# The first four heads of an attention and mixer kernel loaded in pairs, k and q side by side in the partitions; last output chunk in columns of 384 and 128

## The chip, the cores and the metric

The kernel runs on one core of one Trainium2 chip. The metric is device time in microseconds (us). Some kernels here also show a slower state, with a lower granted TensorE clock, and fast runs are compared only with fast runs. In the profile the engines are PE (TensorE matmul), PEld (its weight load), ACT (ScalarE), DVE (VectorE), POOL (GpSimd) and SP (SyncE); "SPq" and "ACTq" are their sequencers, which issue transfers.

## The reference

Block-causal attention (8 batches, 8 heads, 576 positions, 64 columns per head, blocks of 64), then a mixer layer over tokens and one over channels:

```python
scores = 1 / sqrt(64) * q @ k.T          # masked where the query's block is before the key's
x = softmax(scores) @ v                  # heads put side by side: 8 x 576 x 512
h = relu(x.transpose(0, 2, 1) @ w_tok1) @ w_tok2
u = x + h.transpose(0, 2, 1)
out = u + relu(u @ w_ch1) @ w_ch2        # w_ch1 512 x 1536
```

## The kernel before

The program is a list of operations with dependencies and estimated costs. A search with a seeded random generator picks an order, which is then emitted; each engine works through its own list. Only what the change touches is shown.

The first four heads of k and q are loaded as float32 by the two hardware queues (SP and ACT), cast to bf16, and transposed in 32x32 blocks by VectorE. All later ones come through POOL's software queue, which casts on the way.

```python
def load_qk(b, hg, after=[]):
    first = b == 0 and hg == 0
    parts = ((0, NB // 2), (NB // 2, NB))          # two halves of the columns
    for n, (src, raw, dst) in enumerate(((k, kraw[i], kT[i]), (q, qraw[i], qT[i]))):
        hbm = src[b, 4 * hg : 4 * hg + 4].rearrange("h (p k) d -> (h p) (k d)", p=32)   # 4 heads = 128 partitions
        st = stage[0][:, 1152 * n : 1152 * (n + 1)]
        ...
        for f, (k0, k1) in enumerate(parts):
            if first:                              # 128 x 576 floats: 288 KB
                queue.dma_start(out=st[:, D * k0 : D * k1], in_=hbm[:, D * k0 : D * k1])   # SP or ACT
                cast(o, raw2[:, D * k0 : D * k1], st[:, D * k0 : D * k1])                  # ACT or DVE
            nc.vector.transpose(dst..[:, k0:k1], raw2..[:, k0:k1])                         # 128 x 288 int32
```

(The emit functions are shown inlined.) The first score group covers all four heads at once; heads 2 and 3 use two spare PSUM banks and are read by two exps of 512 columns. While TensorE waits in the head of the kernel, small matmuls on zeros ("fillers") keep it busy:

```python
P.add("PE", WARM * 0.36, emit, ...)               # 16 matmuls of 512 columns on zeros
for n in range(KEEP):                             # fillers of 256 columns, used if a gap allows
    P.add("PE", 0.11, emit, ..., at=5.0 + 0.12 * n, until=20.0, quick=True)
```

The last output chunk is computed, added and stored in two parts:

```python
for cols in (slice(0, 256), slice(256, 512)) if last else (slice(0, 512),):
    ...  # 12 matmuls into a bank, add of u by DVE, store by SP
```

The softmax here doesn't subtract the row's maximum and nothing guards it: scores larger than these inputs give would overflow.

## Time and profile before

| | before |
|---|---|
| time, three runs | 307.05 us median (306.29 to 307.42) |
| span of the profiled run | 304.3 us |
| PE busy, share of the chain of waits | 98%, 95% |
| first score, first exp, first channel matmul | 8.24, 8.92, 26.82 |
| PE end, end of the span | 300.96, 304.26 |

The timeline of the queue of ACT shows the cost of issuing; the columns are start, length, engine, line, operation, destination <- source, count, and in brackets the idle time before it and what ended it:

```profile
0.74 0.41 ACTq L380 DMA_DIRECT2D gT<-in_k_dram  x1
1.18 0.46 ACTq L380 DMA_DIRECT2D gT<-in_q_dram  x1
1.67 1.28 ACT L344 ACT_TABLE_LOAD   x1 [1.67 <-PEq L1139]
```

ACT issues two loads at about 0.44 each, then loads its table. The staging buffer bears the name gT, whose memory it borrows. The view by stretches of time has, for each stretch, the busy time of five engines with their instructions, the granted clock, the busy share of the DMA engines (packet times added up, so it can exceed 1), and GB/s:

```profile
2.00:3.50 1.50, 1.50 (x5) 0.61 (x4) 1.16 (x6) 1.15 (x2) 1.50 (x3) 1.00 0.92 313
3.50:5.00 1.50, 1.50 (x7) 0.59 (x5) 0.43 (x3) 0.20 (x1) 1.50 (x4) 1.00 1.00 383
5.00:7.00 2.00, 2.00 (x15) 1.21 (x14) 1.39 (x3) 1.85 (x4) 2.00 (x4) 1.00 1.29 175
```

The four loads move at 383 GB/s between 3.5 and 5. After that the rate is 175 GB/s.

### The profile page before, as it was taken

The numbers are of one execution on the slowest core, as the hardware profiler recorded it, in microseconds if no ns is written. First come the engines' busy times: TensorE is split into PE (matmuls) and PEld (weight loads), VectorE is DVE, ScalarE is ACT, GpSimd is POOL, SyncE is SP. The second block draws the span as 40 slices with busy tenths as digits, with TensorE's granted clock in tenths as the row PEclk, the third lists the DMA queues.
The fourth block names the chain that finished last, engine by engine and source line by source line (L and its number), as shares of the span: only waits on it lengthen the run. The fifth ranks groups of instructions, "written<-read, shape, count | busy, mean of one in ns | idle before, by whom it ended". The sixth has DMA issues, their size and how long they took to land.

```text
span 304.3 us, 7056 instructions
## 1 busy us (share of the span) xinstructions
PE 296.9 (98%) x2999; PEld 160.7 (53%) x3034; DVE 155.5 (51%) x380; ACT 164.6 (54%) x233; POOL 62.1 (20%) x96
## 2 busy tenths in 40 slices
PE   8999999999999999999999999999999999999995
PEld 4575456465454564555554564645446545555443
DVE  5566539989595599584987253615023021010112
ACT  5887855677855756875557856324413503615300
POOL 9766454702610602600140000000000000000000
PEclk9999999999999999999999999999999999999999
DMA  8999999995982998975193002033113222100133
GB/s 202 179 196 209 200 191 187 220 216 91 142 121 44 161 119 139 189 46 60 54 107 88 2 2 53 18 95 97 36 32 140 46 80 49 43 26 2 69 138 106
DMA packets 64383, 31.94 MB, mean 105 GB/s; under 512 B 53088, under 2 KB 55008, under 8 KB 64352
## 3 DMA queue, kind: packets, MB, share of 16 engines
q0 software_dynamic: 44320, 17.34, 48.9%
q1 hardware_dynamic: 19744, 13.57, 17.1%
q10 hardware_dynamic: 288, 0.59, 0.5%
q8 instruction: 23, 0.38, 0.5%
q14 instruction: 8, 0.07, 0.1%
HBM read 35.85 MB, written 9.44 MB: 149 GB/s over the span
## 4 chain that ended last, share of the span: by engine, by line
PE 95%; DMA 2%; issue 1%; DVE 1%; ACT 0%; ACTq 0%
PE mm L1031 31%; PE mm L947 28%; PE mm L555 10%; PE sc L508 10%; PE mm L736 6%; PE mm L829 4%; PE mm L974 4%; DMA gT<-in_q_dram 2%; PE mm L860 1%; PE mm L332 1%; PE mm L780 0%; PE mm L910 0%; DVE qT L393 0%; PE mm L1023 0%; PE mm L765 0%
## 5 line engine op out<-in xcount | busy, mean ns | idle before, releaser
L527 ACT ACTIVATE e_sb<-sc 128x1024 bf16<-128x1024 f32 x95 | 92.5, 1028 | 26.3 <-PE sc L508 24.5
L947 PE MATMUL mm<-uT,wc_sb 128*128 128x512 bf16 x384 | 91.2, 380 | 0.1
L1031 PE MATMUL mm<-wc_sb,gT 128*128 128x512 bf16 (+1 forms) x372 | 89.4, 372 | 1.5 <-issue 0.5
L722 ACT ACTIVATE gT<-mm 128x512 bf16<-128x512 f32 x74 | 44.2, 597 | 63.1 <-PE mm L947 62.8
L947 PEld LDWEIGHTS <-wc_sb 128*128 128x128 bf16 x384 | 41.9, 114 | 39.3 <-issue 3.9
L1031 PEld LDWEIGHTS <-gT 128*128 128x128 bf16 x396 | 36.9, 98 | 40.8 <-issue 3.3
L1056 DVE TENSOR_TENSOR o_sb<-mm,u_sb 128x512 f32<-128x512 f32 (+1 forms) x29 | 19.5, 672 | 74.5 <-PE mm L1031 74.3
L422 POOL DMA_DIRECT2D v<-in_v_dram x45 | 37.2, 839 | 35.3 <-PE sc L508 23.6
L508 PE MATMUL sc<-qT,kT 32*128 32x64 bf16 (+4 forms) x744 | 35.4, 281 | 0.5 <-DVE qT L393 0.5
L555 PEld LDWEIGHTS <-e_sb 128*128 128x128 bf16 x896 | 31.1, 97 | 8.0 <-issue 3.6
L555 PE MATMUL mm<-v,e_sb 128*128 128x65 bf16 x896 | 33.9, 193 | 0.1
L583 DVE TENSOR_TENSOR x_sb<-mm,rinv 128x320 bf16<-128x320 f32 x64 | 31.0, 491 | 2.0
L724 DVE TENSOR_SCALAR gT<-mm 128x512 bf16<-128x512 f32 x22 | 15.2, 689 | 15.9 <-PE mm L947 15.7
L844 DVE TENSOR_TENSOR u_sb<-mm,x_sb 128x512 bf16<-128x512 f32 x28 | 18.0, 686 | 10.2 <-PE mm L829 9.0
L393 DVE STREAM_TRANSPOSE qT<-qraw 128x288 int32<-128x288 int32 x32 | 21.6, 706 | 3.0 <-PE sc L508 2.1
L393 DVE STREAM_TRANSPOSE kT<-kraw 128x288 int32<-128x288 int32 x32 | 20.9, 703 | 4.3 <-DMA kraw<-in_k_dram 1.7
L508 PEld LDWEIGHTS <-kT 32*128 32x128 bf16 x752 | 12.3, 93 | 19.8 <-issue 16.7
L736 PE MATMUL mm<-x_sb,w_sb 128*128 128x512 bf16 (+1 forms) x98 | 18.0, 314 | 0.3
L533 DVE MEMSET e_sb<- 64x128 uint32 (+1 forms) x72 | 10.5, 153 | 14.7 <-ACT e_sb L527 11.4
L373 POOL DMA_DIRECT2D qraw<-in_q_dram x15 | 8.3, 552 | 42.2 <-DVE qT L393 28.5
L577 DVE RECIPROCAL rinv<-mm 128x5 f32<-128x5 f32 x64 | 11.4, 185 | 7.4 <-PE mm L555 6.7
L722 ACT ACTIVATE aT<-mm 128x512 bf16<-128x512 f32 (+1 forms) x15 | 8.1, 543 | 12.3 <-PE mm L736 12.3
(66 smaller groups left out, 175.6 us busy)
## 6 DMA issues: line engine op xcount, KB each, us to landing
out_dram<-o_sb SPq DMA_DIRECT2D x15, 512.0 KB, 2.9
kraw<-in_k_dram POOLq DMA_DIRECT2D x15, 288.0 KB, 7.7
qraw<-in_q_dram POOLq DMA_DIRECT2D x15, 288.0 KB, 7.2
v<-in_v_dram POOLq DMA_DIRECT2D x28, 128.0 KB, 6.9
wc_sb<-in_moe_w_ch_dram POOLq DMA_DIRECT2D x8, 192.0 KB, 7.1
wc_sb<-in_moe_w_ch_dram POOLq DMA_DIRECT2D x3, 512.0 KB, 10.4
out_dram<-o_sb SPq DMA_DIRECT2D x10, 128.0 KB, 2.3
v<-in_v_dram POOLq DMA_DIRECT2D x15, 64.0 KB, 6.1
```

The costliest lines, as they stand in the source:

```text
L393: nc.vector.transpose(dst[:, 0:S, :] .rearrange("p s e -> p (s e)") .bitcast(I32) .rearrange("p (a k) -> p k a", k=NB)[:, k0:k1], raw2.bit ...
L422: nc.gpsimd.dma_start(out=dst, in_=src)
L508: nc.tensor.matmul(out=home(n)[:, c0 : c0 + w], lhsT=kT[i][r, j0 : j0 + 128, par], rhs=qT[i][r, i0 : i0 + w, par], start=(par == 0), stop= ...
L527: nc.scalar.activation(dst, sc[SC.index(note["pool"])][:, :, 0:n], EXP, scale=scale)
L555: nc.tensor.matmul(out=u[:, I, 0:65], lhsT=w, rhs=vt[:, J, head, 0:65], start=(J == 0), stop=(J == I),)
L583: nc.vector.tensor_tensor(out=xt[:, :, 64 * head : 64 * head + 64], in0=u[:, :, 0:64], in1=ri.to_broadcast([128, 5, 64]), op=MULT,)
L722: nc.scalar.activation(dst, src, RELU)
L736: nc.tensor.matmul(out=bank_of(bank)[:, w * n : w * n + w], lhsT=wt[:, tt : tt + 255 : 2], rhs=xt[:, c, cols], start=(c == 0), stop=(c == 4),)
L844: nc.vector.tensor_tensor(out=ut[:, si, :], in0=bank_of(bank), in1=xt[:, si, :], op=ADD)
L947: nc.tensor.matmul(out=bank_of(bank), lhsT=wc1_sb[:, m, channels(cc)], rhs=uT[b % 2][:, :, m, :], start=(m == 0), stop=(m == NDM - 1),)
L1031: nc.tensor.matmul(out=ps, lhsT=gt[:, cc, c0 : c0 + 128], rhs=wc2_sb[:, cc, cols], start=(cc == 0 and not turned), stop=(cc == NDC - 1),)
L1056: nc.vector.tensor_tensor(out=dst, in0=ps, in1=(ut if mixed else ut[:, si, :])[:, cols], op=ADD)
```

## The change

The intent is to let the first two heads start before the other two have arrived. A buffer of 128 partitions holds k of two heads in one half and their q in the other, so one cast serves both; the loads become eight of 64 partitions, the transposes eight of 64 partitions. The four-head score group falls away. The rest: a new seed, the fillers' estimates, and the columns of the last chunk.

```diff
-        rnd = random.Random(0)
+        rnd = random.Random(4)
-        P.add("PE", WARM * 0.36, emit, ...)
+        P.add("PE", WARM * 0.33, emit, ...)
-                ... at=5.0 + 0.12 * n, until=20.0,
+                ... at=5.2 + 0.12 * n, until=20.0,
+    def load_first_qk():
+        done = [[], []]
+        half = NB // 2
+        rows = slice(0, 64), slice(64, 128)
+        for f, (raw, sides) in enumerate(((kraw[0], ((k, kT[0]), (q, qT[0]))), (qraw[0], ((q, qT[0]), (k, kT[0]))))):
+            ...
+            for c in range(2):
+                cols = slice(D * k0, D * k1)
+                for n, (src, _) in enumerate(sides):
+                    def emit_load(o, ...):
+                        hbm = src[0, 2 * f : 2 * f + 2].rearrange("h (p k) d -> (h p) (k d)", p=32)
+                        queue = nc.sync if o.engine == "SP" else nc.scalar
+                        queue.dma_start(out=st[rows[n], cols], in_=hbm[:, cols])
+                    loads.append(P.add(("SP", "ACT")[n], 0.45, emit_load, (), prio - 30, xfer=0.39))
+                ...  # one cast of 128 x 576, heads 0 and 1 on ACT
+                for n, (_, dst) in enumerate(sides):
+                    ...  # transpose raw[rows[n]] into dst[rows[f]], 64 x 288 int32
...
-                if j == 0 and n == 0:
-                    ...  # one score group of four heads, two spare banks
+                note = {}
+                op = score_set(0, parts, heads, ready[j], prio + 0.1 * n, [(SC, note)])
+                these = [exp(dst, width, op, note, prio + 0.1 * n, urgent=2)]
...
-            for cols in (slice(0, 256), slice(256, 512)) if last else (slice(0, 512),):
+            for cols in (slice(0, 384), slice(384, 512)) if last else (slice(0, 512),):
```

## The prediction

> **What bounds the kernel now.** I read the page's busy shares first, then the chain of waits, then the timeline of three stretches: the first 22 us, the hand-over at 19 to 27 us, and the last 6 us.
>
> ```profile
> PE 296.9 (98%) x2999; PEld 160.7 (53%) x3034; DVE 155.5 (51%) x380; ACT 164.6 (54%) x233; POOL 62.1 (20%) x96
> ...
> PE 95%; DMA 2%; issue 1%; DVE 1%; ACT 0%; ACTq 0%
> ```
>
> TensorE (PE) is busy 98% of the span and carries 95% of the chain that ends last. Busy is not proof, so I checked the pace in the timeline: 512-column matmuls start about 0.216 us apart from 21 us to 301 us, and the only larger steps after 24 us are switches between 32-row score matmuls and full ones (about 0.1 us more) and steps of exactly two paces, where a record is missing. So from about 20 us on PE runs a fixed list of work back to back. A change can then win only by (a) starting that list earlier, (b) shortening what follows the last matmul, or (c) changing the list. How the list starts stands in the timeline:
>
> ```profile
> 4.80 1.24 ACT L353 CAST kraw<-gT 128x576 bf16<-128x576 f32 x2 [1.63 <-DMA gT<-in_k_dram]
> ...
> 5.50 1.29 DVE L393 STREAM_TRANSPOSE kT<-kraw 128x288 int32<-128x288 int32 x2 [1.42 <-ACT kraw L353]
> ...
> 6.19 1.25 ACT L353 CAST qraw<-gT 128x576 bf16<-128x576 f32 x2 [0.15 <-DMA gT<-in_q_dram]
> ...
> 6.90 1.29 DVE L393 STREAM_TRANSPOSE qT<-qraw 128x288 int32<-128x288 int32 x2
> ...
> 8.24 0.32 PE L508 MATMUL sc<-qT,kT 32*128 32x320 bf16 x2 [0.46 <-DVE qT L393]
> ...
> 8.92 0.60 ACT L653 ACTIVATE e_sb<-mm 128x512 bf16<-128x512 f32 x1 [1.48 <-PE mm L508]
> ```
>
> (start, length, engine, line, operation; in brackets the idle time before it and its releaser.) The reader is to see a serial chain: load of k lands, cast, four transposes on VectorE (DVE) one after the other, first score matmul at 8.24, first exp at 8.92. From there ScalarE (ACT) is busy without a break (5.00 of 5.00 us in 10-15 and in 15-20) until the last exp of the first batch:
>
> ```profile
> 19.10 1.96 ACT L527 ACTIVATE e_sb<-sc 128x1024 bf16<-128x1024 f32 x2
> ...
> 26.82 2.78 PE L947 MATMUL mm<-uT,wc_sb 128*128 128x512 bf16 x12
> ```
>
> The last score group starts at 19.13, as soon as a score buffer is free, and from it to the first channel matmul at 26.82 PE is full. So the head of the kernel is: chain to the first score, then ACT, then PE for good. The end:
>
> ```profile
> 300.34 1.46 SPq L1067 DMA_DIRECT2D out_dram<-o_sb x2
> 301.00 0.42 DVE L1056 TENSOR_TENSOR o_sb<-mm,u_sb 128x256 f32<-128x256 f32 x1 [0.89 <-PE mm L1031]
> ```
>
> PE ends at 300.98, a 256-column add takes 0.42, the last store goes out at 301.45 and lands 1.7 us later (303.15), and the span closes at 304.3.
>
> **What the Trainium skill says.** "DMA: Bandwidth & Descriptors", Anatomy of one DMA: a fixed cost of about 2.0 us and a part that grows with the bytes. The trace agrees: 128 KB stores land 1.7 to 2.2 us after issue. Its section Rules for kernel authors says that two transfers to disjoint partition halves gain no bandwidth, since they share the same 16 engines. So I give the paired loads no extra bandwidth, only a better order. "VectorE: DVE Perf Modes", Why `tensor_reduce` can't reduce along partition axis: each of the 128 lanes is its own pipeline that streams along the free dimension. I take from this that a transpose of 64 partitions costs what one of 128 does; no run shows it yet. "ScalarE: Activation LUTs", What ACT_TABLE_LOAD costs: 1283 ns; the trace has 1.28 us.
>
> **Part 1, the paired loads (the head).** Before: four loads of 288 KB (k and q, two halves of the columns), four casts, four transposes, and then all four heads are ready. After: eight loads of 144 KB; each buffer holds k of two heads in 64 partitions and their q in the other 64. So there are still four casts of 128x576, but eight transposes of 64x288, and heads 0 and 1 are ready after two casts and four transposes.
>
> - Landing of the first pair. In half-microsecond windows the two hardware queues had moved 0.34 MB by 3.0 us and 0.70 MB by 4.0 us. The 0.59 MB of k had thus moved by about 3.7, and it landed at 4.6 to 4.8 (issued at 0.74, 3.9 and 4.0 to landing): a lag of about 1.0. The first pair is 0.29 MB, moved by about 2.9, so it lands near 3.9.
> - ACT is free. It now issues four loads instead of two at about 0.44 each, so its table load starts at 2.5 instead of 1.67 and, with 1.28 + 0.20 for the warm-up, ACT is free at 4.0. First cast 4.0 instead of 4.80. The second pair lands near 4.75 and its cast is done near 5.45, before its transposes are due.
> - DVE. First transpose 0.70 after the cast starts, as before (5.50 - 4.80): 4.70. Its memsets end at 4.08, so it is free. Four at 1.29 / 2 = 0.645 end at 7.28; first score near 7.35 instead of 8.24. The filler matmuls before it (8 instead of 13 by the instruction order, 0.11 each, from 6.2) end at 7.1 and don't delay it. Shift: **0.87 us**.
> - Heads 2 and 3. Their four transposes end at 7.28 + 2.58 = 9.9. PE first wants them when the second exp frees its buffer: first exp 7.35 + 0.68 = 8.03, two exps at 0.95 each, so 9.93. Just in time, and ACT has a third exp queued, so about 0.5 us of slack remains.
> - ACT stretch. Before, one four-head group filled two spare banks and was read by two exps of 512 columns (pace 0.49 each); now these are one exp of 1024 (pace 0.95). No gain, no loss: ten exps' worth and six small ones stand between first exp and last score group in both, 19.13 - 8.92 = 10.2 us. So the last score group starts near 18.25 and the channel matmuls near 25.95.
>
> **Part 2, the new search seed.** It reorders everything else. By the instruction order the matmuls are the same in number and width (score 752, value 960, channel 384 + 444), only fillers fall from 28 to 21, all of them within the ACT stretch. Runs of score matmuls are 59 in both, so the switch cost is equal. Worth 0, give or take 0.3.
>
> **Part 3, last chunk in 384 + 128.** PE: 12 x (0.162 + 0.056) = 2.6 us against 24 x 0.109 = 2.6: nothing. The last add goes from 0.42 to about 0.29 (0.27 per 256 columns from 0.69 and 0.42): 0.13. But the 384 add (0.56) ends only 0.1 before PE's end, so its store of 192 KB is issued then and lands near 2.1 after PE's end; before, the last landing was 303.15 - 300.98 = 2.17 after. Gain 0.0 to 0.1.
>
> **What takes some back.** The weight and input stream on POOL's queue is full until about 66 us (the profile page's DMA row is 9 in the first eight slices), so its landings don't move when PE does. Before: the last first-layer weight landed at 29.83 and was needed near 31.0; the last v of the second batch landed at 44.03 and its first use started at 44.20. With the new order, adding up the same landing steps (one k load of 1.35 now comes after that v), it lands near 42.7, and PE should want it near 42.6. So a stall of 0 to 0.2 there; I take 0.1.
>
> Sum: 307.05 - 0.87 - 0.05 + 0.1 = **306.2 us**.
>
> **Rivals.**
> - *The DMA stream absorbs the head gain.* For it: a full DMA row until 66 us and a margin of 0.2 us at 44. Against: no PE wait on a DMA after 21 us stands in the waits before, and the new order moves the needed loads up (the second batch's last k load of heads 0-3 has one weight load of 1.0 us fewer before it). If true: 306.9 to 307.2.
> - *DVE becomes the bound of the head.* Eight transposes instead of four are 2.6 us more DVE work before 10 us. If the 64-partition ones were slower than 0.645, or the second pair's loads late, exp 4 would wait: each 0.1 us per transpose costs 0.4 on the first score. At 0.75 the head gain would halve: 306.6.
> - *The first pair lands as late as all of k did* (queues interleaved): first cast at 4.8 and no gain in the head: 307.0.
> - *The new order packs better or worse* in the PE-bound stretch: for it, a different seed; against it, PE has no stall there that could be removed. At most 0.5 either way.
>
> **Range and chances.** Head gain 0.4 to 1.1, tail 0 to 0.2, stream and order -0.5 to +0.3; the three times of before spread over 1.1 us (306.29 to 307.42), so a median of as many runs is good to 0.4. Range 305.2 to 307.2. Two per cent are 6.1 us; nothing here is near that.
>
> **What would show it.** Right: first score matmul at 7.2 to 7.6; 64-partition transposes of the same 0.70 us each; ACT without a gap from 8.0 to about 20; first channel matmul at 25.8 to 26.2; then the same pace to the end, PE ending 0.8 us earlier and the end 3.2 to 3.3 us after PE's. Wrong: a first cast later than 4.3, an ACT gap near 10 us for heads 2 and 3, a PE wait near 30 or 42 us for a load, or a PE end that is not earlier though the first score is.

## The result

The first runs of the changed kernel took 315.68, 308.15, 308.40 and 315.14 us (median 311.77), against 306.9 for the kernel before. Two were slow; a fifth run took 308.21, fast. Its fast runs are 1.0045 times as long as the fast runs of before (95% interval 1.0021 to 1.0069). Such a ratio is the mean time of one kernel's fast runs over that of the other's of the same rounds, so it is not quite the ratio of the medians. In a later job, on another occasion, four runs were all fast: 308.13 to 308.69, ratio 1.0059 (1.0038 to 1.0080). I read the fast trace of that job, "the repeat", against before, and the first, slow trace.

| us | before | predicted | repeat (fast) | first trace (slow) |
|---|---|---|---|---|
| ACT free for the first cast | 3.16 (cast at 4.80, when k had landed) | 4.0 | 4.67 | 4.67 |
| second piece of the first pair landed | | 4.75 | 6.14 | 6.31 |
| first score | 8.24 | 7.35 | 8.42 | 8.59 |
| first exp | 8.92 | 8.03 | 10.19 | 10.52 |
| first channel matmul | 26.82 | 25.95 | 28.13 | 35.68 |
| from there to PE's end | 274.14 | about 274.2 | 274.62 | 274.62 |
| PE's end to the end | 3.30 | 3.2 to 3.3 | 3.61 | 3.60 |

The timeline of ACT in the repeat:

```profile
0.74 1.20 ACTq L377 DMA_DIRECT2D gT<-in_q_dram  x2
1.97 1.26 ACTq L377 DMA_DIRECT2D gT<-in_k_dram  x2
3.27 1.28 ACT L344 ACT_TABLE_LOAD   x1 [3.27 <-issue]
...
4.67 0.66 ACT L353 CAST kraw<-gT 128x576 bf16<-128x576 f32 x1
6.22 0.67 ACT L353 CAST kraw<-gT 128x576 bf16<-128x576 f32 x1 [0.89 <-DMA gT<-in_k_dram]
8.38 0.67 ACT L353 CAST qraw<-gT 128x576 bf16<-128x576 f32 x1 [1.49 <-DMA gT<-in_q_dram]
9.61 0.67 ACT L353 CAST qraw<-gT 128x576 bf16<-128x576 f32 x1 [0.55 <-DMA gT<-in_q_dram]
10.19 2.85 ACT L556 ACTIVATE e_sb<-sc 128x1024 bf16<-128x1024 f32 x3
```

Three of the four casts wait for a load, and the first exp stands behind the last of them, though its scores began at 8.42. The rates of the repeat by stretches of time (columns as before):

```profile
3.50:5.00 1.50, 1.50 (x6) 0.54 (x4) 0.36 (x2) 1.49 (x3) 1.50 (x3) 1.00 1.27 216
5.00:7.00 2.00, 2.00 (x14) 1.15 (x12) 1.50 (x3) 1.00 (x2) 2.00 (x4) 1.00 1.22 204
```

216 GB/s where before had 383; POOL's stream is already under way here, from 3.61. Between 2 and 3.5, ahead of it, the repeat has 261 and before 313. The timeline of PE and of DVE in the repeat:

```profile
8.42 1.09 PE L537 MATMUL sc<-qT,kT 32*128 32x64 bf16 x16 [1.00 <-DVE qT L393]
9.44 0.94 PE L332 MATMUL mm<-zeros 128*128 128x256 bf16 x7
11.26 0.63 PE L537 MATMUL sc<-qT,kT 32*128 32x512 bf16 x4 [0.88 <-ACT e_sb L556]
...
28.13 1.05 PE L958 MATMUL mm<-uT,wc_sb 128*128 128x512 bf16 x4
```

```profile
5.36 0.71 DVE L393 STREAM_TRANSPOSE kT<-kraw 64x288 int32<-64x288 int32 x1 [1.27 <-ACT kraw L353]
6.08 0.71 DVE L393 STREAM_TRANSPOSE qT<-kraw 64x288 int32<-64x288 int32 x1
```

PE stands still from 10.38 to 11.26 for an exp; VectorE starts its transposes 0.72 apart. From the first exp on nothing is lost: 28.13 - 10.19 = 17.94 to the first channel matmul, 26.82 - 8.92 = 17.90 before. The slow trace has this clock row (40 slices, tenths of full speed) on its page, and these lines in PE's timeline:

```profile
PEclk9855999999999999999999999999999999999999
```

```profile
9.61 0.94 PE L332 MATMUL mm<-zeros 128*128 128x256 bf16 x7
11.59 0.63 PE L537 MATMUL sc<-qT,kT 32*128 32x512 bf16 x4 [1.04 <-ACT e_sb L556]
```

The clock records give half speed from 13.92 for 17.07 us. In the traces the fast change costs 2.10 us: 1.31 up to the first channel matmul, 0.48 from there to PE's end, 0.31 after it. (The timed medians, 308.35 against 306.52 in that job, differ by 1.8.)

### The profile page after: what moved, and what is told of

Its sections match the earlier page's. It is cut to its first block, busy times and chain, and to the rows that moved or that the text cites. A ratio compares the mean times of both kernels' runs of the same rounds, so it can differ in the third digit from the quotient of the medians.

```text
span 313.9 us, 7086 instructions
## 1 busy us (share of the span) xinstructions
PE 307.7 (98%) x3027; PEld 164.6 (52%) x3027; DVE 159.7 (51%) x387; ACT 163.8 (52%) x229; POOL 62.1 (20%) x96
## 4 chain that ended last, share of the span: by engine, by line
PE 92%; DVE 2%; DMA 2%; ACT 1%; SPq 1%; issue 0%; ACTq 0%
PE mm L1042 29%; PE mm L958 27%; PE sc L537 10%; PE mm L584 10%; PE mm L747 6%; PE mm L840 4%; PE mm L985 3%; DMA gT<-in_q_dram 2%; DVE qT L422 1%; DVE x_sb L612 1%; PE mm L871 1%; SPq L377 1%; ACT e_sb L556 1%; PE mm L791 1%; PE mm L332 0%; DVE kT L422 0%
## 5 line engine op out<-in xcount | busy, mean ns | idle before, releaser
L1042 PE MATMUL mm<-wc_sb,gT 128*128 128x512 bf16 (+2 forms) x396 | 91.3, 373 | 0.0
L958 PE MATMUL mm<-uT,wc_sb 128*128 128x512 bf16 x384 | 90.1, 380 | 0.0
L733 ACT ACTIVATE gT<-mm 128x512 bf16<-128x512 f32 x76 | 45.4, 597 | 61.7 <-PE mm L958 60.8
L1067 DVE TENSOR_TENSOR o_sb<-mm,u_sb 128x512 f32<-128x512 f32 (+2 forms) x29 | 19.5, 671 | 72.6 <-PE mm L1042 58.7
L537 PE MATMUL sc<-qT,kT 32*128 32x64 bf16 (+4 forms) x752 | 38.9, 290 | 1.3 <-ACT e_sb L556 1.3
L584 PEld LDWEIGHTS <-e_sb 128*128 128x128 bf16 x896 | 34.1, 101 | 9.6 <-issue 4.1
L584 PE MATMUL mm<-v,e_sb 128*128 128x65 bf16 x896 | 36.9, 199 | 0.1
L606 DVE RECIPROCAL rinv<-mm 128x5 f32<-128x5 f32 x64 | 11.4, 183 | 18.1 <-PE mm L584 17.8
L422 DVE STREAM_TRANSPOSE qT<-qraw 128x288 int32<-128x288 int32 x30 | 19.7, 704 | 0.6 <-PE sc L537 0.5
L735 DVE TENSOR_SCALAR gT<-mm 128x512 bf16<-128x512 f32 x20 | 13.8, 690 | 9.7 <-PE mm L958 9.4
L417 POOL DMA_DIRECT2D kraw<-in_k_dram x15 | 8.2, 552 | 30.8 <-DVE kT L422 28.4
```

The costliest lines, as they stand in the source:

```text
L422: nc.vector.transpose(dst[:, 0:S, :] .rearrange("p s e -> p (s e)") .bitcast(I32) .rearrange("p (a k) -> p k a", k=NB)[:, k0:k1], raw2.bit ...
L537: nc.tensor.matmul(out=home(n)[:, c0 : c0 + w], lhsT=kT[i][r, j0 : j0 + 128, par], rhs=qT[i][r, i0 : i0 + w, par], start=(par == 0), stop= ...
L584: nc.tensor.matmul(out=u[:, I, 0:65], lhsT=w, rhs=vt[:, J, head, 0:65], start=(J == 0), stop=(J == I),)
L733: nc.scalar.activation(dst, src, RELU)
L958: nc.tensor.matmul(out=bank_of(bank), lhsT=wc1_sb[:, m, channels(cc)], rhs=uT[b % 2][:, :, m, :], start=(m == 0), stop=(m == NDM - 1),)
L1042: nc.tensor.matmul(out=ps, lhsT=gt[:, cc, c0 : c0 + 128], rhs=wc2_sb[:, cc, cols], start=(cc == 0 and not turned), stop=(cc == NDC - 1),)
```

## The experiments

All keep the order of the kernel they start from unless said otherwise: only what is emitted differs. In one job the kernels share 11 runs of the kernel before, whose medians were 306.52, 306.44, 306.35 and 306.26; none of those 44 runs showed a granted clock under 0.998. All results were correct.

Theory at the start: the half loads are slow or collide with POOL's stream, their lateness reaches the first exp through ACT's order, and the gap on PE costs the clock. Rivals: eight issues instead of four; the early v loads; another order; the split of the tail.

**The changed kernel again.**

> The changed kernel again, to get a trace in the fast state and to count its slow runs. Late-piece theory: in the fast state too the last quarter of the paired loads lands near 9.8 us, its cast stands before the first exp on ScalarE, so the first exp starts near 10.5 us (8.92 before) and the time is 308.2. Rival (the head is only late in the slow run, the fast runs lose their 1.3 us in the reordered body or the tail): first exp at 8.0 to 9.0 in the fast trace. Two of five runs were slow; about the same share here.

308.13, 308.30, 308.39, 308.69, all fast, where two in five had been slow. Last piece down at 9.53, first exp 10.19, first channel matmul 28.13. The late-piece theory holds.

**More fillers in the gap.** The edit: `for _ in range(1 if emitted[0] <= 8 else 3 if emitted[0] <= 12 else 2)` around the filler matmul.

> The changed kernel in the same order, but the fillers that follow the first two score groups are doubled or tripled (13 real ones become 30), so that TensorE does not idle for 1.3 us while it waits for the first exp. Clock theory (the slow state is the TensorE clock that falls to half after a window with too much idle time): no slow run in five rounds, fast time unchanged at 308.2 (within 0.5). Rival (slow runs come from the chip and not from the idle gap): slow runs stay at two in five.

Six runs, 308.89 to 309.37, none slow; ratio 1.0079 (1.0064 to 1.0094). The fillers cost 0.6 of the fast time, a little more than the 0.5 that I had allowed, and the first channel matmul came at 28.9. No slow run in six is what the clock theory wants, but the unfilled kernel had none in four of the same job, so this run alone doesn't prove it.

**The first two v loads of POOL's stream swapped.** The edit: two entries of the order exchanged.

> The changed kernel in the same order, but the first two v loads on POOL's queue change places, so the queue begins with a 128-row load as the kernel before does. In the slow trace the software queue's small packets begin at 3.5 us, in the kernel before at 4.5. If that early start is what slows the paired loads: the last of them lands at about 7.5 instead of 9.8, first exp near 9, and 1 us is won in the fast state (307.2). If the eight issues themselves are the cause (0.6 us each, the last ends at 3.5 instead of 1.64): landing stays above 9 and the time at 308.2.

316.35, 315.54, 307.82, 315.69; three of four slow. In its trace, a slow run whose half clock began at 11.25, the half loads landed between 3.65 and 9.59, as without the swap, and the first exp came at 10.25. Which v load goes first isn't the cause. The early start itself was not tested here, since the stream still began at 3.54.

**Four loads of 64 x 1152 floats instead of eight of 64 x 576.**

```diff
+ if c == 1: return
+ cols = slice(0, 1152)
  queue.dma_start(out=st[rows[n], cols], in_=hbm[:, cols])
```

> The changed kernel in the same order, but the eight loads of 64 partitions by 576 columns are issued as four of 64 by 1152. If the number of loads is the cause: issues end near 2.0, all four land by 6.5, first cast near 4.8, first exp near 8.9, and the time falls from 308.2 to about 306.8. If the early small packets are the cause, landing stays near 8 to 9 and the time near 308.

Fast runs 308.75 to 309.00 (and one slow, 317.26), ratio 1.0073 (1.0052 to 1.0094). The loads landed at 4.80, 6.08, 7.42 and 9.05. With the issues of before and the bytes per load of before (288 KB), the loads are still late, so the number of issues isn't the cause of that. (Each of the four took 0.56 to 0.82 us to issue, against 0.39 to 0.46 before.)

**The kernel before with its four first loads cut along the partitions.**

```diff
- queue.dma_start(out=st[:, D * k0 : D * k1], in_=hbm[:, D * k0 : D * k1])
+ r = slice(64 * f, 64 * f + 64)
+ queue.dma_start(out=st[r], in_=hbm[r])
```

> The kernel before in its own order with its own four casts and transposes; only the four first loads are cut along the partitions (64 by 1152) instead of along the columns (128 by 576), same bytes, same number, same queues. Half-port theory[...]: k lands at 6 or later instead of 4.6 to 4.8, q at 7.4 to 9.1 as in the changed kernel with four loads, first score 1.3 to 3 us later, time 308 to 310 fast. Rival (the changed kernel's loads are late because of POOL's stream or its order, not because of their shape): landings stay at 4.6 to 6.2 and the time at 306.5.

Fast runs 310.44 and 310.85, ratio 1.0132 (1.0109 to 1.0155), two of four slow. Both fast runs show a clock of 0.994, so up to 1.9 us of the 4 (an estimate, 0.006 x 309) may be lost clock. The trace is of a slow run, but its half clock began at 10.86, after the last of these loads (8.99). The page's DMA issues (KB each, us from issue to landing), then a stretch of time:

```profile
gT<-in_q_dram ACTq DMA_DIRECT2D x1, 288.0 KB, 6.1
gT<-in_q_dram SPq DMA_DIRECT2D x1, 288.0 KB, 7.6
```

```profile
3.50:5.00 1.50, 1.50 (x8) 0.58 (x6) 0.43 (x3) 0.00 (x0) 1.50 (x4) 1.00 0.99 252
```

Before, those two took 5.0 and 4.7, at 383 GB/s. POOL's stream sent its first packet at 4.74 here, so nearly all of this stretch is without it. The shape alone brings 252 of 383 GB/s, in the kernel before and with nothing else of the program changed. This is the cleanest evidence that loads of 64 partitions are slow; the records call it the half-port theory, but no run looks at ports. The packets changed with the shape (4608 bytes, 2304 before). The later-stream run below has 2304 again and 258 GB/s, so their size isn't the cause.

**The kernel before with eight loads of 128 x 288, k first.**

```diff
- queue.dma_start(out=st[:, D * k0 : D * k1], ...)
+ mid = D * (k0 + k1) // 2
+ for queue, c in ((nc.sync, slice(D * k0, mid)), (nc.scalar, slice(mid, D * k1))):
+     queue.dma_start(out=st[:, c], in_=hbm[:, c])
```

> The kernel before in its own order; the four loads of 128 by 576 become eight of 128 by 288, issued in the order k first half, k second half, q first half, q second half, each half split over both queues. Half-port theory: eight loads over all 128 partitions are not late; the first half of k lands near 3.8, the last of q still near 6.1, first cast near 4.0, first score near 7.6 instead of 8.24, time 0.4 to 0.7 lower than before. Rival (eight loads are late because they are eight): the last lands after 8 and the time rises by 1 or more.

Fast runs 308.34 to 310.12, ratio 1.0076 (1.0058 to 1.0095), two of seven slow. Half a miss: k landed at 3.56 to 4.46 and ACT cast it from 4.01, but q landed at 6.48, 6.98, 9.19 and 9.59 (a slow run again, half clock from 10.94). ACT's timeline:

```profile
7.06 0.67 ACT L353 CAST qraw<-gT 128x576 bf16<-128x576 f32 x1 [1.82 <-DMA gT<-in_q_dram]
9.67 0.67 ACT L353 CAST qraw<-gT 128x576 bf16<-128x576 f32 x1 [1.93 <-DMA gT<-in_q_dram]
```

No theory so far said this, since these loads span all 128 partitions. What they share with the changed kernel's last pieces is that they are still under way when POOL's stream begins (4.50 here). A new theory: what hasn't moved by then shares the 16 engines with that stream's packets, most of them of 128 bytes, and crawls.

**The kernel before with the last chunk in 384 and 128.**

> The kernel before in its own order; only the last chunk is emitted in columns of 384 and 128. In the changed kernel 3.6 us pass from the last matmul to the end, before 3.3. Tail theory (the split costs 0.3): 3.6 here too, time up by 0.3. Rival (the store order of the new seed costs it, the split itself is neutral as predicted): 3.2 to 3.3, time within 0.1.

305.86 to 306.98, ratio 0.9993 (0.9977 to 1.0008). Neutral. Its trace has 3.16 from PE's end to the end instead of 3.30, and one wait of 0.44 near 59 us that the other traces of this order lack.

**The kernel before without the fillers behind the first score group.**

> The kernel before in its own order, without the 15 filler matmuls that stand after the first score (the 13 ahead of it stay). Clock theory: TensorE idles in the gaps between score groups, so some runs fall to half clock for 10 to 20 us and take 313 to 316, the rest stay at 306.5. Rival (slow runs have nothing to do with TensorE's idle time): no slow run.

311.18 to 312.20, all with a clock of 0.973 to 0.978; ratio 1.0162 (1.0144 to 1.0180). The page's clock row and PE's timeline:

```profile
PEclk9758999999999999999999999999999999999999
```

```profile
10.49 0.63 PE L511 MATMUL sc<-qT,kT 32*128 32x64 bf16 x8 [1.09 <-ACT e_sb L530]
11.64 0.62 PE L511 MATMUL sc<-qT,kT 32*128 32x512 bf16 x4 [0.52 <-ACT e_sb L530]
```

The head came as before (first score 8.25), the gaps are of 1.1 and 0.5 us, half clock lasted from 12.21 to 25.87, and 5.0 us were lost. I had expected some runs at 313 to 316 and the rest at 306.5; instead all four lost the clock, for less time. This shows that these two gaps, 1.6 us of idle time close together, suffice to lose it.

**The changed kernel with POOL's stream 2.45 us later.** The edit: `for _ in range(6): make_identity(nc, ident)`.

> The changed kernel in the same order, but GpSimd makes the identity matrix six times instead of once (about 2.45 us more), so that its software stream of v, k, q and weights starts that much later. Collision theory (half loads still unfinished when the software stream's many small packets begin share the 16 DMA engines with them and crawl): packets of the stream begin near 6 instead of 3.5, all eight half loads are down by 6.8 to 7.4 instead of 9.5 to 9.9, last cast starts at 7.4 or earlier, first exp at 8.3 to 8.8 (10.19 in the repeat), time 306.6 to 307.4. Rival (the 64-partition shape alone makes them late): the last still lands at 9 or later, first exp at 9.9 or later, time 308.0 to 308.6. Third: the loads are early but v and weights are now late, first exp under 9 and time still 308.

308.21 to 308.98, ratio 1.0063 (1.0034 to 1.0092). DMA issues, a stretch of time, and a wait in PE's timeline:

```profile
gT<-in_k_dram ACTq DMA_DIRECT2D x2, 144.0 KB, 4.6
gT<-in_q_dram SPq DMA_DIRECT2D x2, 144.0 KB, 4.8
```

```profile
3.50:5.00 1.50, 1.50 (x5) 0.45 (x3) 0.36 (x2) 1.49 (x3) 1.29 (x4) 1.00 0.98 258
```

```profile
39.94 1.02 PE L1043 MATMUL mm<-wc_sb,gT 128*128 128x512 bf16 x3 [0.26 <-DMA wc_sb<-in_moe_w_ch_dram]
```

The stream's first packet came at 6.14 instead of 3.61, and the last half load landed at 7.86 instead of 9.53 (in the repeat those two groups took 5.6 and 6.3). The collision is shown and is worth 1.7 us of landing. The first exp moved from 10.19 to 9.21, 0.4 later than expected, since the first score still came at 8.54. But the rate before the stream begins is 258 GB/s, not 383: shape and collision both act. And the time did not move. The first channel matmul came 0.77 earlier, and waits behind it took 0.83 back: the stretch to PE's end grew from 274.62 to 275.45. Against the usual step between the same matmuls, PE is about 0.42 late at the weight shown above, 0.19 near 44.5, where a v load landed at 44.50, and twice 0.12 with no cause found. The third outcome.

**The casts of heads 2 and 3 on VectorE.** The edit: `nc.vector.tensor_copy` for f == 1, the two casts placed in the order where their transposes begin.

> The changed kernel, but the two casts of heads 2 and 3 are done by VectorE and stand in its order where their transposes begin, so the first exp has no cast behind a late load ahead of it on ScalarE. Theory (the last cast, which waits for the load that lands at 9.5, blocks the exps in ScalarE's order): first exp at 9.0 to 9.2 instead of 10.19, although that load still lands at 9 to 10; PE gap ahead of the second score run shorter; first channel matmul 27.1 to 27.5 (28.13), time 307.2 to 307.7. Rival (exps are held by the scores or by heads 2 and 3, not by the cast): first exp moves but the first channel matmul stays at 28.0 or later, time 308.0 to 308.6.

313.81 to 315.84, ratio 1.0265, every run with a clock of 0.972 to 0.976. The timelines of ACT and of PE:

```profile
9.30 2.90 ACT L564 ACTIVATE e_sb<-sc 128x1024 bf16<-128x1024 f32 x3 [2.21 <-PE sc L545]
```

```profile
11.13 0.28 PE L332 MATMUL mm<-zeros 128*128 128x256 bf16 x1
12.77 0.68 PE L545 MATMUL sc<-qT,kT 32*128 32x64 bf16 x8 [1.35 <-DVE kT L400]
```

The first exp came at 9.30, 0.67 after the first score (8.63). So it was the cast in ACT's order that held it in the repeat; that part of the theory is shown. But the casts then lengthened VectorE's chain, PE waited at 11.4 to 12.8 instead, and half clock came in all four runs. The time that I expected, 307.5, was far off.

**The eighths of the kernel before, with POOL's stream 1.47 us later.**

> The kernel before with eight loads over 128 partitions, k first, as in the quarter run, and GpSimd's stream 1.47 us later (identity four times). Collision theory: k down by 4.5 as in the quarter run, q down by 5.6 to 6.0 instead of 9.6, casts at 4.0, 4.6, 5.5, 6.1, first score at 7.5 to 7.9 (8.24 before), first exp 8.2 to 8.6, first channel matmul 26.2 to 26.6, time 305.7 to 306.2, ratio 0.998. Rival (the later issue of the q loads itself, or the later stream of v and weights, costs it): first score 8.2 or later or value matmuls that wait, time 306.5 to 308.

Fast runs 307.13 to 309.97 (one slow, 313.06), ratio 1.006 (1.002 to 1.010). A miss on the gain, a hit on the collision: q landed at 5.85 to 6.98 instead of 6.48 to 9.59. But that isn't earlier than the 5.87 and 6.17 of before; the first score came at 8.63, and PE waited 0.52 at 26.7 for a transpose of a later k. Between 3.5 and 5 the rate was 279 GB/s (383 before), but 324 against 313 between 2 and 3.5; whether loads of 128 x 288 are slower as such stays open.

**The kernel before with the stream 0.98 us later.**

> The kernel before with GpSimd's stream 0.98 us later (identity three times) and nothing else. Collision theory: the q halves, 6.17 and 5.87 before, land at 5.4 to 5.7, third cast at 5.9 (6.19), first score at 7.95 to 8.1 (8.24), time 306.1 to 306.4, ratio 0.999. Control for the cost of a later stream: if v and weights are then short, first score is earlier but the first channel matmul is not, and the time is 306.5 to 307.

306.20 to 308.20, ratio 1.0021 (0.9993 to 1.0049). q landed at 5.77 and 6.04, only 0.1 earlier, and the stream's first packet came at 4.97, as before (4.98): while the large loads run, the stream gets no earlier start by being issued earlier. In its trace the clock was full only from 6.66 (4.36 before), so the warm-up matmuls ended late and the first score came at 8.86. Nothing is won here.

**The kernel before with the new seed.**

> The kernel before with the search's seed of the changed kernel (4 for 0) and nothing else: the head is the old one, the order of the rest another. Theory (the 0.8 us after the first channel matmul belongs to the seed and the order it picks, not to the new head): stretch from the first channel matmul to TensorE's end other than 274.14 by more than 0.1, or the 3.30 from there to the end other by more than 0.1; time 306.8 to 307.4. Rival (the order differs only in its head, and the seed is worth nothing): 274.1 to 274.2, 3.2 to 3.3, time 306.2 to 306.7.

306.40 to 308.36, ratio 1.0014 (0.9989 to 1.0039). From the first channel matmul to PE's end 274.13, as with the old seed; from there to the end 3.55 instead of 3.30. Its trace has one more wait that delays the first channel matmul to 27.88:

```profile
27.31 0.63 PE L508 MATMUL sc<-qT,kT 32*128 32x64 bf16 x16 [1.07 <-DVE kT L393]
```

**The changed kernel with the old seed.**

> The changed kernel with the search's old seed (0 for 4). First exp stays at 10.0 to 10.5 and the first channel matmul near 28.1 by every theory, since loads and casts are as in the changed kernel. Theory (seed and order made the 0.8): the stretch to TensorE's end comes to 274.0 to 274.3 and the rest to 3.2 to 3.4, time 307.5 to 307.9. Rival (the pairs in the head made it): 274.5 to 274.7 and 3.5 to 3.7, time 308.1 to 308.5. Either can show half clock; only fast runs count.

Fast runs 308.27 to 308.98 (one slow, 317.07), ratio 1.0061 (1.0037 to 1.0085). First exp 9.95, stretch to PE's end 274.63, and 4.35 from there. So the seed by itself doesn't make the 0.48: that stretch is 274.14 and 274.13 with the old head, 274.62 and 274.63 with the new one. But the last two are no single cost of the new head. Against the usual step between the same matmuls, all traces of the changed kernel's order have PE late by 0.08, 0.20 and 0.24, in value matmuls 19 to 25 us after the first channel matmul. With the old seed these are gone, and it is late by 0.11, 0.18, 0.08 and 0.12 at other places, 34 to 79 us after it. The split's run, with old head and old order, reached 274.64 by its one wait. So the 0.48 lies in waits of the order that the search picked; that the head makes them is not shown. What follows PE's end is no clearer: other orders have more than the 3.30 of before (3.55, 3.61, 4.35), but the old order alone ranges from 3.16 to 3.85 over its variants, and the changed kernel's from 3.56 to 4.08.

**The later stream, and the transposes of heads 2 and 3 in the order q, q, k, k.**

> The changed kernel with GpSimd's later stream, and the four transposes of heads 2 and 3 in the order q, q, k, k instead of q, k, q, k. Theory (two transposes into the same tile and rows can overlap, and a change of tile or rows ends the overlap): starts 0.55 to 0.60 apart within q, q and k, k, about 0.73 between them, the four in 2.6 instead of 2.9 us. Rival (64 partitions are slow whatever the order): 0.72 to 0.74 apart throughout.

One run, 308.15, state unknown. DVE's timeline with q, k, q, k (the run with the later stream), then with q, q, k, k:

```profile
8.52 0.71 DVE L394 STREAM_TRANSPOSE qT<-qraw 64x288 int32<-64x288 int32 x1
9.25 0.71 DVE L394 STREAM_TRANSPOSE kT<-qraw 64x288 int32<-64x288 int32 x1
```

```profile
8.31 1.25 DVE L396 STREAM_TRANSPOSE qT<-qraw 64x288 int32<-64x288 int32 x2
9.57 1.25 DVE L396 STREAM_TRANSPOSE kT<-qraw 64x288 int32<-64x288 int32 x2
```

Two of a kind start 0.55 apart, a change of kind costs 0.71, and the four take 2.51 instead of 2.89 us. The order sets the pace, not the 64 partitions. In this run rows and tile change together, but a change of tile alone costs nothing: transposes of all 128 partitions that go from kT to qT or back start 0.55 to 0.56 apart, like those that stay (medians of 127 and 168 pairs in all traces).

**A version that beats both** did not come out of this. Without the collision the changed kernel still has its first score at 8.36 to 8.54, later than the 8.24 of before, and a later stream costs weights. Splitting the last chunk is neutral.

## Why the prediction was wrong

*PE runs a fixed list, so the head decides: right.* From the first channel matmul to PE's end, traces of one order agree within 0.02 us, apart from single waits. *ACT's stretch unchanged: right*, 17.94 against 17.90 from first exp to first channel matmul.

*"It now issues four loads instead of two at about 0.44 each": mis-sized.* They took 0.62 each, so ACT was free at 4.67 and the first transpose started at 5.36 instead of 4.70: 0.66.

*"The second pair lands near 4.75": this step failed, and the landings carry the case.* I had the first halves right (3.9; 3.59 and 4.22), but I took the byte rate of 128-partition loads for 64-partition ones. The second pair landed at 4.87 and 6.14. So the four pieces of heads 0 and 1 were down at 6.14, when before all four heads were down at 6.17. The rule that I cited (no bandwidth from disjoint halves) I read as "no gain"; the runs show a loss, 252 of 383 GB/s at equal size. The Trainium skill has a possible reason on another page, "SBUF — State Buffer", Door 1: The DMA port swizzle: partitions 0 to 63 reach 8 of the 16 DMA ports. The measured 0.66 of the rate agrees in direction. But here loads to both halves were in flight together, and no run looks at ports, so the reason is not shown.

*"Just in time" for heads 2 and 3: failed.* Their last pieces landed at 9.53. Two causes are shown: the slow shape, and the collision with POOL's stream (7.86 without it). That stream's first packet came at 3.61 here against 4.98 before. Where it isn't issued later on purpose, it comes at 3.34 to 3.61 with eight half loads and at 4.74 to 5.41 with four loads of 288 KB; why is not shown. I had set the second pair's landing by bytes alone.

*Four transposes at 0.645 each: mis-sized.* They start 0.73 apart, 0.34 for four. The skill's "VectorE: DVE Perf Modes", section Two Vector instructions with no wait between them, says that an instruction whose input or output starts in another group of 32 partitions than the last one's begins only when all earlier ones have finished. The trace agrees: the changed kernel alternates partitions 0 and 64, at 0.73, and the reordered run drops to 0.55. The duration itself, 0.71, is that of 128 partitions, as I said.

*Sum for the first exp.* Predicted 8.03, measured 10.19. The first score is 1.07 late. Two chains end there almost together. The second pair, down at 6.14, is cast at 6.22 and transposed from 6.92 to 8.37, for a score at 8.42. The late first cast and the slower transposes (0.66 + 0.34) would by themselves have given about 8.3, an estimate from the same trace. So repairing one of the two alone would have won 0.1 or nothing. The other 1.09 is the last cast, which waits for its load and stands before the exp in ACT's order: 8.42 + 0.68 would have been 9.10. I had not looked at the order of ACT at all, only at when heads 2 and 3 were needed.

*Seed 0 give or take 0.3, tail 0.0 to 0.1 of gain: mis-sized.* The stretch to PE's end grew by 0.48 and what follows by 0.31. The 0.48 lies in waits of the order that the search picked, as the run with the old seed shows; in the repeat the two largest are of 0.20 and 0.24 us, in value matmuls near 51 and 53 us, while VectorE works on transposes. What ties them to the new head, if anything does, is open. For the 0.31 there is only a suspicion: a 512 KB store issued 2.7 us before PE's end in the repeat (7.0 before) lands among the last ones. The split's trace shows a small gain behind PE's end (3.16 against 3.30; the times show none), and both differences are smaller than the range over one order's variants.

*The stall of 0.1 in the DMA stream:* not seen.

*What I left out: the clock.* Counting PE's busy time in the 3.41 us windows that the clock's changes mark (half clock lasted 13.65, 17.07, 20.48 or 23.89 us in the traces, whole multiples of 3.413), over the traces of before, of the change and of all 15 experiments:

| least busy window in the head, before any loss | runs | clock |
|---|---|---|
| 0.04, 0.05, 0.53, 0.57, 0.60, 0.63 | eighths, rows cut, no fillers, swapped v, casts on VectorE, first trace | half after that window |
| 0.64 to 0.69 | four loads, repeat, new seed | kept |
| 0.77 to 0.97 | before (0.81) and seven others | kept |

So the change's gap near 10 to 11.5 us takes its window to the edge, and by these traces whether a run loses 7 us depends on where the windows fall. That is read from the traces; only the effect of the gaps was tested, by the runs with more and with fewer fillers. Before, the least busy was 0.81. Ends of matmuls are modelled, so the edge between 0.63 and 0.64 isn't as sharp as it looks.

The nearest of my rivals was "the first pair lands as late as all of k did", with a first cast at 4.8. The first cast did come at 4.67, but because of ACT's own issues: the first pair was down at 4.22. "VectorE becomes the bound" had a part (0.73 a transpose, where I had named 0.75). I gave the two 306.6 to 307.0, since I took each alone. Two slips in the prediction's figures change nothing: by its own times the shift is 0.89 (8.24 - 7.35), not 0.87, and the DMA row of the page begins with 8, not 9. The fixed cost that it cites from "Anatomy of one DMA" is there stated for POOL's software path, while the stores that it was compared with go by SP's queue.

## What to carry to other kernels

Cutting a load along the partitions to get one half's data first can bring that half no earlier than the whole came before: take the rate of the new shape and size from a run, not only the bytes, and look at which other stream starts while the load is under way. Look also at what stands behind a consumer of late data in its engine's order: here the first exp waited for a cast that it doesn't need. In a kernel bound by TensorE, count the idle time of its head before you widen a gap there: here windows of 3.41 us with up to 1.23 us idle kept the clock and those with 1.26 or more lost it, 308 against 315 us.

## What the Trainium skill lacked or had wrong

- "TensorE: Matmul & The Clock Gate", section HAM oscillation: it gives the rule as no idle gaps over about 3.4 us. Here gaps of 1.1 and 0.5 us in one window were enough; windows busy 0.63 or less lost the clock, 0.64 or more kept it. Its section A second HAM failure mode does name frequent short idle times between groups of matmuls, but gives no size. Its table in Part 1 has the clock full again after one busy window of about 3.4 us; here half clock stayed 13.65 to 23.89 us, four to seven windows, with PE busy 0.91 or more of each.
- "DMA: Bandwidth & Descriptors", Rules for kernel authors: the rule against disjoint halves says that there is nothing to gain. That row lacks the loss: 252 against 383 GB/s for 288 KB loads, two in flight. The loss stands on another page, "SBUF — State Buffer", Door 1, as 196 GB/s for partitions 0 to 63 against 328 for all 128, at 1 MiB.
- No page that I read has a figure for hardware-queue loads that meet a software stream of small packets: the last load landed at 9.53 with it and at 7.86 when the stream began later.
- No page that I read gives the issue time of a load by its shape: 0.62 us for 64 x 576 floats on ACT against 0.39 to 0.46 for 128 x 576 on SP and ACT.
